# A hand-woven issue order against one computed by a list schedule in the builder and pinned

## The chip, the cores and the metric

The kernel runs on one core of one Trainium2 chip. The metric is the device time of one execution in microseconds, taken as the median over the runs of a kernel. Five engines matter here. PE does the matmuls, DVE (the vector engine) does element-wise work, ACT (the scalar engine) does copies and scaling, and POOL and SP mostly issue DMAs. Each engine works through its own list of instructions. So when the next instruction on the list has to wait, everything behind it waits too, ready or not. The Trainium skill, "Perfetto Trace Analysis", section "Per-engine timelines", says the same of ACT, DVE and POOL, whose queues it calls strict FIFO, and the traces here agree: one held list of ACT cost it 16.8 us.

## The reference, cut to what matters

```python
def reference(...):
    x = A_x                                            # 2048 x 1024
    g = sigmoid((x * gate_w).sum(-1, keepdims=True))
    a = _A_ref(x, ...)    # S5: a complex linear recurrence over 2048 steps,
                          #     h = Lam_bar * h + B_bar x,  y = 2 Re(C h) + x * Dskip
    b = _B_ref(x, ...)    # H3: kv = shift_conv(k) * v ; y = irfft(rfft(kv) * rfft(ssm_k))
                          #     + kv * ssm_D ; result q * y   (q is x)
    return g * a + (1 - g) * b
```

The kernel does the long convolution `b` with matmuls against sine and cosine tables, in eight rounds of 128 channels each. The recurrence `a` is done in four blocks of 512 time steps with eight groups of 128 states each, that is 32 units, called S5 units below.

## The kernel before

One round of the convolution goes through many hands. DVE prepares `kv` (shift convolution), a DMA stores and reloads it in another layout, PE does a first stage into PSUM, ACT copies that out as `zkv`, PE forms the spectrum, ACT copies it out as `kv`, DVE multiplies (`product`, result `pp`), PE transforms back (`inverse`), ACT copies that out as `qq`, 16 DMAs per round move `qq` into the layout `zb`, PE does a last stage (`final`), ACT copies it out as `cv`, and POOL stores it to `pB_scr` in memory. The S5 units are the filler that was put between these steps by hand:

```python
def evac(eng, o, i_, scale=None):            # copy a PSUM tile out
    if eng == "V":
        nc.vector.tensor_copy(o, i_)
    else:
        nc.scalar.copy(o, i_)
        todo = list(late); late.clear()
        for f in todo: f()                   # the zb stores wait for the next ACT copy

def zb_store(zb, qq, q):
    for i in range(4):
        k2 = 4 * q + i
        nc.scalar.dma_start(out=zb[k2:128:16]..., in_=qq[:, i]...)     # issued by ACT

# ... (cut: tables, parameters)
APU = [1, 2, 2, 2, 2, 2, 2, 3]               # S5 units per round, chosen by hand
for u in range(NU):                          # eight rounds
    na = 4 * APU[u]
    slots = [(i * na) // 12 for i in range(13)]
    # ... fill() advances the S5 stream by slots[pos+1]-slots[pos] steps
    if u > 0:
        # ... (cut)
        for q in range(4):
            stage1(ka, z, 0, q, "V" if q == 1 else "A")    # which engine copies: by hand
            if q == 1: fill()
        inverse(*pend, "A")
        # ... (cut)
    for q in range(4):
        spec(z, kv, q, 0, "A"); fill()
        spec(z, kv, q, 1, "A")
        pp_new = product(kv)
        next(kvg, None)                      # one step of the next round's kv
        if zb_prev is not None and q in (0, 1): final(zb_prev, u - 1, q, "A")
        if pend is not None: inverse(*pend, "A")
        pend = (pp_new, zb, q)
        fill()
# then the last part: C is transposed in and scaled (4 ACTIVATEs and 2 adds for each
# of 8 groups), S5 blocks 2 and 3, and 16 output tiles: 512 matmuls of 512 columns
```

Of the kernel before, what the change touches and what calls it, by code (L numbers as in the profile page):

```python
# [9 lines left out]
ALU = mybir.AluOpType  # L10
# [7 lines left out]
TB_MAX = 512  # L18


@with_exitstack
def kernel(
# [59 lines left out]

# [4 lines left out]
    bW = b.enter_context(tc.tile_pool(name="bW", bufs=1, side="right"))  # L87
    bpsum = b.enter_context(tc.tile_pool(name="bpsum", bufs=3, space=bass.MemoryType.PSUM))

# [28 lines left out]

    late = []

    def evac(eng, o, i_, scale=None):
        if eng == "V":
            nc.vector.tensor_copy(o, i_)
        else:
            nc.scalar.copy(o, i_)  # L125
            todo = list(late)
            late.clear()
            for f in todo:
                f()

    kv_tiles = {}

    def kv_load(job, pool):
        c0 = job * 128
        kT = pool.tile([128, S], BF16, name="kT")
        nc.sync.dma_start_transpose(out=kT, in_=kf[:, c0:c0 + 128])
        vT = pool.tile([128, S], BF16, name="vT")
        nc.sync.dma_start_transpose(out=vT, in_=vf[:, c0:c0 + 128])
        kv_tiles[job] = (kT, vT)

    def kv_steps(job, pool):
        c0 = job * 128
        kT, vT = kv_tiles.pop(job)
        acc = pool.tile([128, S], BF16, name="acc")
        nc.vector.tensor_scalar(out=acc, in0=kT, scalar1=skc[:, job, 0:1], scalar2=None, op0=ALU.mult)  # L145
        for j in range(1, KS):
            tmpj = pool.tile([128, S], BF16, name="tmpj")
            if j in (1,):
                nc.scalar.activation(out=tmpj[:, 0:S - j], in_=kT[:, 0:S - j], func=ACT.Identity,  # L149
                                     scale=skc[:, job, j:j + 1])  # L150
            else:
                nc.vector.tensor_scalar(out=tmpj[:, 0:S - j], in0=kT[:, 0:S - j], scalar1=skc[:, job, j:j + 1],
                                        scalar2=None, op0=ALU.mult)
            nc.vector.tensor_tensor(out=acc[:, j:S], in0=acc[:, j:S], in1=tmpj[:, 0:S - j], op=ALU.add)  # L154
            yield
        nc.vector.tensor_tensor(out=acc, in0=acc, in1=vT, op=ALU.mult)
        nc.gpsimd.dma_start(out=kv_scr[c0:c0 + 128, :], in_=acc)
        yield

    def load_A(src, u, name):  # L160
        t = bA.tile([128, NG, 128], BF16, name=name)
        nc.gpsimd.dma_start(out=t, in_=src[u * CH:(u + 1) * CH, :].rearrange("(g c) (n m) -> (c n) g m", c=8, m=128))
        return t

    def load_K(u):
        return load_A(B_ssm_k, u, "ka")

    def fix_K(u, ka):
        nc.vector.tensor_tensor(out=ka[:, :, 0], in0=ka[:, :, 0], in1=sdz[:, u * NG:(u + 1) * NG], op=ALU.add)  # L169

    def stage1(a, z, w, q, eng):
        ps = bpsum.tile([128, 4, 256], F32, name="ps")
        for i in range(4):
            nc.tensor.matmul(ps[:, i, :], lhsT=a[:, 4 * q + i, :], rhs=t1v, start=True, stop=True)  # L174
        evac(eng, z[:, :, w, :, 32 * q:32 * q + 32].rearrange("p k r (g c) -> p k r g c", c=8),
             ps.rearrange("p g (k r c) -> p k r g c", r=2, c=8))

    def spec(z, kv, q, h, eng):
        ps = bpsum.tile([128, 2, 2, 2, CH], F32, name="ps")
        for i in range(2):  # L180
            k2 = 4 * q + 2 * h + i
            nc.tensor.matmul(ps[:, i], lhsT=fC[:, k2, :], rhs=z[:, k2], start=True, stop=False)  # L182
            nc.tensor.matmul(ps[:, i, :, 0, :], lhsT=fS[:, k2, :], rhs=z[:, k2, :, 1, :], start=False, stop=False)  # L183
            nc.tensor.matmul(ps[:, i, :, 1, :], lhsT=fN[:, k2, :], rhs=z[:, k2, :, 0, :], start=False, stop=True)  # L184
        evac(eng, kv[:, 2 * h:2 * h + 2], ps)

    def product(kv):
        t1 = bW.tile([128, 4, 2, CH], BF16, name="t1")
        t2 = bW.tile([128, 4, 2, CH], BF16, name="t2")
        pp = bW.tile([128, 4, 2, CH], BF16, name="pp", bufs=2)  # L190
        nc.vector.tensor_tensor(out=t1, in0=kv[:, :, 0], in1=kv[:, :, 1], op=ALU.mult)
        nc.vector.tensor_tensor(out=t2[:, :, 0, :], in0=kv[:, :, 0, 0, :], in1=kv[:, :, 1, 1, :], op=ALU.mult)
        nc.vector.tensor_tensor(out=t2[:, :, 1, :], in0=kv[:, :, 0, 1, :], in1=kv[:, :, 1, 0, :], op=ALU.mult)
        nc.vector.tensor_tensor(out=pp[:, :, 0, :], in0=t1[:, :, 0, :], in1=t1[:, :, 1, :], op=ALU.subtract)
        nc.vector.tensor_tensor(out=pp[:, :, 1, :], in0=t2[:, :, 0, :], in1=t2[:, :, 1, :], op=ALU.add)  # L195
        return pp

    def zb_store(zb, qq, q):
        for i in range(4):
            k2 = 4 * q + i  # L200
            nc.scalar.dma_start(out=zb[k2:128:16].rearrange("s g r c -> s g (r c)"),  # L201
                                in_=qq[:, i].rearrange("p r c -> p (r c)"))

    def inverse(pp, zb, q, eng):
        ps = bpsum.tile([128, 4, 2, CH], F32, name="ps")
        for i in range(4):
            k2 = 4 * q + i
            nc.tensor.matmul(ps[:, i], lhsT=gC[:, k2, :], rhs=pp[:, i], start=True, stop=False)  # L208
            nc.tensor.matmul(ps[:, i, 0, :], lhsT=gN[:, k2, :], rhs=pp[:, i, 1, :], start=False, stop=False)  # L209
            nc.tensor.matmul(ps[:, i, 1, :], lhsT=gS[:, k2, :], rhs=pp[:, i, 0, :], start=False, stop=True)  # L210
        qq = bW.tile([128, 4, 2, CH], BF16, name="qq", bufs=2)
        evac(eng, qq, ps)
        late.append(lambda: zb_store(zb, qq, q))

    def final(zb, u, h, eng):
        ps = bpsum.tile([128, 2, 4, CH], F32, name="ps")
        for i in range(2):
            g0 = 8 * h + 4 * i
            nc.tensor.matmul(ps[:, i], lhsT=tFc, rhs=zb[:, g0:g0 + 4, 0, :], start=True, stop=False)
            nc.tensor.matmul(ps[:, i], lhsT=tFs, rhs=zb[:, g0:g0 + 4, 1, :], start=False, stop=True)  # L220
        cv = bW.tile([128, 8, CH], BF16, name="cv")
        evac(eng, cv, ps.rearrange("p a g c -> p (a g) c"))
        nc.gpsimd.dma_start(out=pB_v[:, 8 * h:8 * h + 8, u * CH:(u + 1) * CH], in_=cv)  # L223


    def load_BT(i):
        nc.sync.dma_start_transpose(out=BTre[i], in_=A_B_re[:, i * 128:(i + 1) * 128])
        nc.sync.dma_start_transpose(out=BTim[i], in_=A_B_im[:, i * 128:(i + 1) * 128])

    def load_xT(tbk, pool):  # L230
        xT_b = pool.tile([128, ND, TB], BF16, name="xT_b")
        for dt_ in range(ND):
            nc.sync.dma_start_transpose(out=xT_b[:, dt_, :],  # L233
                                        in_=xf[tbk * TB:(tbk + 1) * TB, dt_ * 128:(dt_ + 1) * 128])
        return xT_b

    def rot_table(pool, pi):
        ht = pool.tile([128, TB], F32, name="t1")
        nc.vector.tensor_scalar(out=ht, in0=iota_row, scalar1=col(thn, pi), scalar2=None, op0=ALU.mult)
        rq = pool.tile([128, TB], F32, name="t2")  # L240
        nc.vector.tensor_scalar(out=rq, in0=ht, scalar1=MAGIC, scalar2=-MAGIC, op0=ALU.add, op1=ALU.add)
        nc.vector.tensor_tensor(out=ht, in0=ht, in1=rq, op=ALU.subtract)
        nc.scalar.activation(out=rq, in_=ht, func=ACT.Abs)
        nc.scalar.activation(out=TBs[pi], in_=ht, func=ACT.Sin, scale=TWO_PI)
        nc.scalar.activation(out=TBc[pi], in_=rq, func=ACT.Sin, bias=pihalf_col, scale=-TWO_PI)

    def gates(tb, xT_b, psg):
        for tl in range(TT_B):
            for dt_ in range(ND):
                nc.tensor.matmul(psg[:, tl:tl + 1], lhsT=xT_b[:, dt_, tl * 128:(tl + 1) * 128],  # L250
                                 rhs=gwb[:, dt_:dt_ + 1], start=(dt_ == 0), stop=(dt_ == ND - 1))
        s_ = slice(tb * TT_B, (tb + 1) * TT_B)
        nc.scalar.activation(out=gcols[:, s_], in_=psg[:, 0:TT_B], func=ACT.Sigmoid)
        nc.scalar.activation(out=omg[:, s_], in_=psg[:, 0:TT_B], func=ACT.Sigmoid, scale=-1.0)

    hbs = {}
    inits = {}
    bus = {}
# [57 lines left out]
    def drain(gen):  # L316
        for _ in gen:
            pass
# [420 lines left out]
```

## Time and profile before

| | before |
|---|---|
| time, median of 2 runs | 642.45 us (641.56 to 643.35) |
| set-up (to the first spectrum matmul) | 56.3 us |
| middle (to the store of the last `pB_scr` tile) | 367.5 us |
| last part | 217.9 us |
| PE, DVE, ACT busy over the whole | 65%, 65%, 53% |

First come some lines of the page of the kernel before: the busy times, the busy tenths of PE and DVE in 40 slices of the span (9 means 90% or more), and at the end the chain of work that ended last, by engine.

```profile
span 641.7 us, 6317 instructions
...
PE 415.0 (65%) x2201; PEld 218.7 (34%) x2240; DVE 417.8 (65%) x741; ACT 340.2 (53%) x373; POOL 61.6 (10%) x86
...
PE   0204545746835844656876886245967797999996
...
DVE  4927574765964962766976765500999949888331
...
issue 40%; DVE 20%; PE 16%; DMA 10%; ACT 7%; POOL 2%; ACTq 2%; SPq 1%; POOLq 0%; DVEq 0%
```

DVE's row has no stretch of nines until the last part, and PE's only at the very end. In the chain the largest share is "issue", which is time in which an engine waited for nothing that the profile shows.

The table by windows cuts the span at the two landmarks given above. Its columns are the window, its length, then busy us and number of instructions for PE, the weight loads, DVE, ACT and POOL, then the granted clock, the DMA share and GB/s.

```profile
core 0: us, PE busy (x) PEld busy (x) DVE busy (x) ACT busy (x) POOL busy (x), PEclk, DMA share, GB/s
0.00:56.30 56.30, 8.86 (x65) 5.93 (x66) 33.06 (x76) 30.91 (x29) 10.63 (x17) 0.76 0.94 168
56.30:423.80 367.50, 224.93 (x1322) 133.70 (x1343) 241.96 (x435) 205.98 (x237) 32.93 (x36) 0.81 0.40 87
423.80:641.70 217.90, 181.24 (x815) 79.03 (x832) 142.78 (x230) 103.30 (x108) 18.05 (x33) 0.92 0.35 83
```

The set-up is bound by DMA (share 0.94). In the middle, DVE is the busiest engine, yet it is busy for only 241.96 of 367.5 us. So the length of the middle is DVE's work plus 125.5 us of DVE idleness. The same view cuts the last part into three stretches:

```profile
424.00:454.00 30.00, 19.05 (x77) 6.86 (x80) 5.75 (x9) 8.36 (x11) 6.06 (x11) 0.62 1.08 198
454.00:518.00 64.00, 49.51 (x207) 20.94 (x209) 62.88 (x107) 48.71 (x54) 2.15 (x4) 0.95 0.25 48
518.00:642.00 124.00, 112.68 (x535) 51.23 (x544) 74.15 (x115) 46.23 (x45) 9.67 (x18) 0.98 0.22 72
```

These are 30 us with DVE nearly idle and DMA at 1.08 (the share can come out slightly above 1 in a short window), 64 us with DVE full (62.88 busy), and 124 us with PE nearly full.

What DVE waited for in the middle is shown by the view of waits. Its columns are who waited for whom, then us in total, the number of times, and the longest.

```profile
engine line waited for: us in total, times, longest us
DVE acc L145 <- DMA kv_scr<-acc: 28.7, 6, 5.3
DVE ka L169 <- DMA ka<-in_B_ssm_k_dram: 25.9, 6, 6.6
DVE t_3068 L191 <- ACT kv L125: 6.1, 1, 6.1
```

The two largest waits are for DMA round trips: DVE may not start the next `acc` before the store of the last one has left the buffer, and it may not correct `ka` before its load has landed. The rest of the 125.5 us is scattered over many waits of about 6 us and less.

### The profile page before, as it was taken

The page shows a single profiled execution, that of the slowest core. Times are in us where ns is not written, and L with a number is a line of the kernel's source. Part 1 is how long each engine was busy: PE and PEld are TensorE (multiplying, and loading weights), DVE is VectorE, ACT ScalarE, POOL GpSimd, SP SyncE. Part 2 cuts the span into 40 slices and gives each one's busy share as a digit, 9 for nine tenths or more (in the row PEclk, how much of TensorE's full clock was granted, in tenths as well). Part 3 has the DMA queues.
Part 4 walks back from the last instruction along what each step waited for, and adds up shares of the span by engine and source line. Part 5 has one row for each costly group of instructions (what it writes and reads, how often), then busy time and mean ns, then how long its engine had stood idle before and what let it go on. Part 6 is the DMA issues. An engine that isn't in the chain of part 4 may idle for free.

```text
span 641.7 us, 6317 instructions
## 1 busy us (share of the span) xinstructions
PE 415.0 (65%) x2201; PEld 218.7 (34%) x2240; DVE 417.8 (65%) x741; ACT 340.2 (53%) x373; POOL 61.6 (10%) x86
## 2 busy tenths in 40 slices
PE   0204545746835844656876886245967797999996
PEld 0103224423523523434443543112422343444442
DVE  4927574765964962766976765500999949888331
ACT  2867934845645624846646663212888543433431
POOL 4100101101101101001101000040010011100000
PEclk9858687778967967789988978667897999899999
DMA  9992563263254246264233213389920033211211
GB/s 125 232 184 49 132 131 66 66 133 81 67 115 97 53 109 128 57 148 99 59 99 75 50 33 86 63 171 195 175 65 1 1 99 98 88 60 50 83 38 44
DMA packets 113799, 59.41 MB, mean 93 GB/s; under 512 B 89128, under 2 KB 105512, under 8 KB 113768
## 3 DMA queue, kind: packets, MB, share of 16 engines
q1 hardware_dynamic: 86784, 25.18, 20.3%
q0 software_dynamic: 7504, 25.44, 16.2%
q10 hardware_dynamic: 19480, 8.40, 6.0%
q8 instruction: 17, 0.28, 0.2%
q14 instruction: 14, 0.11, 0.1%
HBM read 17.06 MB, written 12.58 MB: 46 GB/s over the span
## 4 chain that ended last, share of the span: by engine, by line
issue 40%; DVE 20%; PE 16%; DMA 10%; ACT 7%; POOL 2%; ACTq 2%; SPq 1%; POOLq 0%; DVEq 0%
PE psy L648 12%; DMA kv_scr<-acc 6%; DVE W L287 4%; PE bu L266 3%; ACT zkv L125 2%; ACTq L201 2%; DVE acc L154 2%; SPq L233 1%; DMA kT<-in_B_k_dram 1%; DMA pB_scr<-cv 1%; PE ps L208 1%; ACT qq L125 1%; POOL pB_scr L223 1%; ACT cv L125 1%; DMA xT_b<-in_A_x_dram 1%
## 5 line engine op out<-in xcount | busy, mean ns | idle before, releaser
L125 ACT CAST kv<-ps 128x1024 bf16<-128x1024 f32 x64 | 63.2, 1018 | 33.9 <-DMA xT_b<-in_A_x_dram 16.8
L208 PE MATMUL ps<-pp,gC 128*128 128x256 bf16 x128 | 37.7, 320 | 65.7 <-DVE pp L195 53.4
L182 PE MATMUL ps<-zkv,fC 128*128 128x512 bf16 x118 | 49.6, 421 | 40.1 <-ACT zkv L125 25.9
L648 PEld LDWEIGHTS <-hb 128*128 128x128 bf16 x512 | 50.6, 99 | 73.3 <-issue 15.2
L125 ACT CAST zkv<-ps 128x1024 bf16<-128x1024 f32 x50 | 48.8, 1016 | 31.8 <-PE ps L174 23.3
L125 ACT CAST qq<-ps 128x1024 bf16<-128x1024 f32 x32 | 32.6, 1019 | 37.3 <-PE ps L210 37.2
L183 PE MATMUL ps<-zkv,fS 128*128 128x256 bf16 x128 | 38.5, 300 | 1.2 <-issue 0.9
L174 PE MATMUL ps<-tab_143,ka 128*128 128x256 bf16 x128 | 21.9, 331 | 26.2 <-DVE ka L169 19.8
L184 PE MATMUL ps<-zkv,fN 128*128 128x256 bf16 x128 | 38.6, 302 | 0.0
L125 ACT CAST bu<-bu 128x1024 bf16<-128x1024 f32 x32 | 32.2, 1007 | 11.4 <-DVE t_4049 L282 4.6
L266 PE MATMUL bu<-xT_b,BTre_68 128*128 128x512 bf16 x32 | 14.5, 453 | 35.8 <-ACT bu L125 17.6
L145 DVE TENSOR_SCALAR acc<-kT,skc 128x2048 bf16<-128x2048 bf16 x8 | 6.0, 753 | 44.6 <-DMA kv_scr<-acc 28.7
L208 PEld LDWEIGHTS <-gC 128*128 128x128 bf16 x128 | 14.3, 112 | 60.4 <-DVE pp L195 60.0
L660 ACT ACTIVATE pbb<-pbb,omg 128x1024 bf16<-128x1024 bf16 x16 | 18.3, 1147 | 30.3 <-DMA pbb<-pB_scr 21.1
L210 PE MATMUL ps<-pp,gS 128*128 128x128 bf16 x128 | 32.1, 251 | 0.0
L209 PE MATMUL ps<-pp,gN 128*128 128x128 bf16 x128 | 32.1, 250 | 0.0
L656 ACT ACTIVATE ga<-psy,gcols 128x1024 bf16<-128x1024 f32 x16 | 17.7, 1104 | 26.1 <-PE psy L648 26.1
L154 DVE TENSOR_TENSOR acc<-acc,tmpj 128x2047 bf16<-128x2047 bf16 (+2 forms) x24 | 29.2, 1217 | 2.9 <-ACT tmpj L149 2.8
L664 DVE TENSOR_TENSOR ot<-m_t,ga 128x1024 bf16<-128x1024 bf16 x16 | 11.0, 688 | 30.6 <-ACT ga L656 30.4
L287 DVE TENSOR_TENSOR_SCAN W<-rv,init_re,pre 128x512 bf16<-128x512 f32 x24 | 30.7, 1278 | 0.0
L287 DVE TENSOR_TENSOR_SCAN W<-rv,init_im,pre 128x512 bf16<-128x512 f32 x24 | 30.2, 1260 | 0.0
L659 ACT ACTIVATE m_t<-dsk,gcols 128x1024 bf16<-128x1024 bf16 x16 | 18.4, 1148 | 20.0 <-DVE ot L664 20.0
(706 smaller groups left out, 1154.2 us busy)
## 6 DMA issues: line engine op xcount, KB each, us to landing
zb<-qq ACTq DMA_DIRECT2D x128, 64.0 KB
ka<-in_B_ssm_k_dram POOLq DMA_DIRECT2D x8, 512.0 KB, 5.5
kv_scr<-acc POOLq DMA_DIRECT2D x8, 512.0 KB, 4.7
va<-kv_scr POOLq DMA_DIRECT2D x8, 512.0 KB, 5.5
pB_scr<-cv POOLq DMA_DIRECT2D x16, 256.0 KB, 3.5
x_tt<-in_A_x_dram POOLq DMA_DIRECT2D x16, 256.0 KB, 3.0
pbb<-pB_scr POOLq DMA_DIRECT2D x16, 256.0 KB, 3.0
out_dram<-ot SPq DMA_DIRECT2D x16, 256.0 KB
```

The lines of the kernel that those rows point to most:

```text
L125: nc.scalar.copy(o, i_)
L154: nc.vector.tensor_tensor(out=acc[:, j:S], in0=acc[:, j:S], in1=tmpj[:, 0:S - j], op=ALU.add)
L174: nc.tensor.matmul(ps[:, i, :], lhsT=a[:, 4 * q + i, :], rhs=t1v, start=True, stop=True)
L182: nc.tensor.matmul(ps[:, i], lhsT=fC[:, k2, :], rhs=z[:, k2], start=True, stop=False)
L183: nc.tensor.matmul(ps[:, i, :, 0, :], lhsT=fS[:, k2, :], rhs=z[:, k2, :, 1, :], start=False, stop=False)
L184: nc.tensor.matmul(ps[:, i, :, 1, :], lhsT=fN[:, k2, :], rhs=z[:, k2, :, 0, :], start=False, stop=True)
L208: nc.tensor.matmul(ps[:, i], lhsT=gC[:, k2, :], rhs=pp[:, i], start=True, stop=False)
L209: nc.tensor.matmul(ps[:, i, 0, :], lhsT=gN[:, k2, :], rhs=pp[:, i, 1, :], start=False, stop=False)
L210: nc.tensor.matmul(ps[:, i, 1, :], lhsT=gS[:, k2, :], rhs=pp[:, i, 0, :], start=False, stop=True)
L266: nc.tensor.matmul(ps[:, r, :], lhsT=BT[dt_][:, pi * 128:(pi + 1) * 128], rhs=xT_b[:, dt_, :], start=(dt_ == 0), stop=(dt_ == ND - 1))
L287: nc.vector.tensor_tensor_scan(out=W[:, r, :], data0=col(rv, pi).to_broadcast([128, TB]), data1=pre[:, r, :], initial=(0.0 if tb == 0 else ...
L648: nc.tensor.matmul(psy[:, dh, :], lhsT=hb[:, r, tl * 128:(tl + 1) * 128], rhs=CT[pi][:, dh * 512:(dh + 1) * 512], start=(pi == 0 and r == ...
```

## The change

The intent is to take the order out of the programmer's hands. Arithmetic, tiles and buffer counts stay. Each operation is described by the engines that may do it with an estimated cost, by what it reads and writes, and by a priority key (the round number with a fraction). A list scheduler in the builder then simulates the engines and buffers. It takes next whatever can start first, and among what can start within 0.1 us of that it takes the lowest key. The kernel's instructions are written out in that order, and at the end each instruction gets an ordering-only dependency on the one before it on the same engine. That last step is the pin. It is needed because the framework's own scheduler may otherwise move independent instructions of one engine past each other. The diff, cut to its core:

```diff
+class Planner:
+    DMA_RATE = 200e3
+    def start_of(self, o, e):                       # earliest start of op o on engine e
+        s = max([self.free.get(e, 0.0)] + [d.end for d in o.deps])
+        for t in o.w:                               # a new tile needs a free buffer
+            ...
+                if len(line) >= n:
+                    if line[-n].left: return None
+                    s = max(s, line[-n].end)
+        return s
+    def run(self, window=0.3, flex=0.0):
+        while ready:
+            ...
+            for e, c in by.items():
+                first = min(s for s, _ in c)
+                s, o = min(((s, o) for s, o in c if s <= first + window),
+                           key=lambda x: (x[1].key + (flex if ... e != next(iter(x[1].eng)) ...), x[1].n))
+                if pick is None or s < pick[0]: pick = (s, o, e)
+            s, o, e = pick
+            c = o.eng[e]
+            ...
+MM = {512: 0.216, 256: 0.108, 128: 0.062}           # us of a matmul by its columns
+def dma(q, kb):
+    return {q: (0.6, kb, 1.0)} if q != "POOL" else {q: (1.0, kb, 1.5)}
-def evac(eng, o, i_, scale=None):
+def evac(o, i_, r, w, cost=1.0, key=None):
+    ...
+    return op({ACTE: cost * 1.0, DVE: cost * 1.15}, fn, r, w, key=key)   # either engine
-            nc.scalar.dma_start(out=zb[k2:128:16]...
+            op(dma("SP", 64), lambda e, ...: nc.sync.dma_start(out=zb.ap[k2:128:16]...
-                nc.scalar.activation(out=t, in_=s_, func=ACT.Identity, scale=col(k_, pi))
+            op({ACTE: 0.98, DVE: 0.36}, f, [raw], [t])                   # C scaling
-    for u in range(NU):        # the hand-woven loop: slots, fill(), pend, late
-        ...
+    for u in range(NU):
+        base = KB0 + KBU * u                        # keys: round number, plus
+        ...
+        for q in range(4):
+            pl.key = base + 0.2 + 0.2 * q           # a fraction for each step
+            spec(...); spec(...); pp = product(kv); inverse(pp, zbs[u], q)
+    for tb in range(2):
+        base = KA0 + KAP * NP * tb                  # S5 units, at 0.4 rounds each
+        ...
+    t_end = pl.emit(window=0.1, flex=0.3)
+    ...
+    last = {}                                       # the pin
+    for ins in list(nc.cur_bb.bb.instructions):
+        prev = last.get(ins.engine)
+        if prev is not None:
+            tc.add_manual_dep(ins, prev.name, mybir.DependencyInfo(
+                mybir.DependencyClass.NoSync, mybir.DependencyReason.DATA), reason="order")
+        last[ins.engine] = ins
```

Three things move besides the order: the `zb` stores go from ACT to SP, PSUM copies may go to ACT or DVE as the planner finds best, and so may the scaling of C. (So may one small job, the first product of the shift convolution: 7 of its 8 instances stayed on ACT.)

## The prediction

> **What bounds the kernel now.** No engine is full: the page gives PE 65%, DVE 65%, ACT 53% of 641.7 us. The table by windows shows three regimes.
>
> - 0 to 56 us, set-up: DMA share 0.95; transposed loads fill the DMA engines.
> - 56 to 418 us, eight convolution rounds (about 46 us each) with S5 blocks woven in by hand: DVE 242 us busy of 362 (67%), ACT 205 (57%), PE 224 at a granted clock of 0.81, DMA 0.39. Nothing saturates; in-order waiting binds. The waits of 131 to 366 us: the inverse on DVE's product (35 us), the spectrum on ACT's zkv (19), ACT on the inverse (24). ACT's queue also issues the 128 zb stores at 0.61 us each, 78 us that the busy figure omits; one of them held ACT for 16.9 us behind the x transposes at 228 to 245.
> - 418 to 642 us: 30 us with DVE idle, DMA at 0.99 (x and C transposes); 64 us bound by DVE (63.3 busy); 130 us bound by PE (a 512-column matmul every 0.22 us, clock 0.98).
>
> **What changes.** Arithmetic, tiles and buffer counts stay. Every engine's order is computed greedily and pinned. PSUM copies can go to ACT (1.02 us) or DVE (1.22 us); C scaling, 32 x 1.15 us on ACT, can go to DVE (estimate 0.4 us, from the 0.75 us twice-as-wide scaling). The zb stores move to SP. The Trainium skill, "DMA: Bandwidth & Descriptors", section "Issuing engines are not separate DMA queues", says that the issuing engine saves only sequencer time; so the saving is ACT's 78 us, not bandwidth. The stores now queue behind SP's transposes, issued at 1.3 us each, sometimes stalling 2 to 5 us.
>
> **Cost.** Middle part: DVE+ACT+issue is 525 us on two engines now, 447 without the issues. DVE's fixed share is about 225 us, so the floor is near 230 us against 362. A greedy order should reach about 80%: 285 us, with some 15 us of tail after the S5 stream. Set-up stays DMA-bound, about 55 us. Last part: the C loads still wait for the tables' memory, so the 30 us gap stays nearly whole. PE needs 512 + 256 matmuls x 0.218 = 168 us there; if C is scaled 40 us in, out(0) can run under in(2): about 205 us against 224.
> Sum: 55 + 285 + 205 = 545. A frozen order amplifies wrong estimates: the planner costs a 512 matmul at 0.216 us where a slow clock gives 0.43, a transpose issue at 0.6 against 1.3, and knows no queue limits. I add 15 us: 560 us, range 530 to 605. Chances: faster 0.93, same 0.04, slower 0.03.
>
> **What would show it.** Round period falls from 46 to 35-38 us; DVE busy in the middle above 80%; no zb store left on ACT's queue; PSUM copies on DVE rise from 14 to several tens; the granted clock in the middle rises above 0.85 as PE idles less; a DVE gap of 20 us or more remains before the last part; PE near-saturated over the last 110 to 130 us.
>
> **What would make it wrong.** zb stores delayed behind transposes on SP, so that qq's two buffers hold ACT and the pinned order spreads this to PE and DVE: 3 to 5 us per round would cost up to 40 us. A pinned order that waits on a late DMA (C loads before out(0), va before stage 1) would show as one long wait on all engines. DVE overloaded by greedily taken copies would show as DVE above 95% with ACT below 50%. Upward surprise: set-up shortened by loading kv before B.

## The result, and the profile after

The kernel with the change took 549.96 us (median of 2 runs, 548.59 to 551.33) against 642.45 us. All ratios in this document are fast runs of one kernel against fast runs of the other in the same rounds, so they are not quite the ratio of the medians quoted. Here the ratio is 0.856 with a 95% interval of 0.8455 to 0.8665.

The lines of the page that answer to those of before:

```profile
span 549.6 us, 6362 instructions
...
PE 389.1 (71%) x2203; PEld 209.1 (38%) x2240; DVE 427.8 (78%) x758; ACT 310.5 (57%) x347; POOL 61.4 (11%) x85
...
PE   0024618877969678879787640766669999999996
...
DVE  4893978999989789899899810099999899997331
...
PE 40%; DVE 26%; DMA 12%; issue 7%; ACT 7%; SPq 6%; POOL 1%; ACTq 0%; DVEq 0%; POOLq 0%
```

DVE's row is now almost only sevens to nines from the fifth slice to 316 us, shortly before the middle ends (333.2 us), and the chain that ended last consists of work (PE 40%, DVE 26%) where it had consisted of "issue" (7%, from 40%). The table by windows, with the same landmarks:

```profile
0.00:52.60 52.60, 7.13 (x32) 4.47 (x33) 34.77 (x88) 30.05 (x34) 10.44 (x16) 0.83 1.06 165
52.60:333.20 280.60, 204.74 (x1357) 125.44 (x1377) 241.65 (x427) 189.98 (x218) 32.43 (x36) 0.90 0.51 112
333.20:549.60 216.40, 177.21 (x814) 79.21 (x830) 151.41 (x244) 90.49 (x95) 18.56 (x34) 0.91 0.38 89
```

| part | before | after | difference |
|---|---|---|---|
| set-up | 56.3 us | 52.6 us | -3.7 us |
| middle | 367.5 us | 280.6 us | -86.9 us |
| last part | 217.9 us | 216.4 us | -1.5 us |

So nearly all of the gain lies in the middle. DVE's busy time there is the same to within 0.3 us (241.96 and 241.65). What fell is its idle time, from 125.5 us to 280.6 - 241.65 = 38.9 us. That is 86.6 us less, which accounts for the whole difference of 86.9 us. Of the 38.9 us that are left, 15.7 are a tail from 317.5 us on, in which DVE has done its part of the rounds and already waits for the last part (12 us of the 125.5 were of that kind before); inside the rounds DVE is now idle for only about 23 us. The view of DVE's waits in the middle shows that the two large ones have gone or shrunk:

```profile
DVE z L385 <- PE ps L468: 6.2, 2, 4.1
DVE ka L459 <- DMA ka<-in_B_ssm_k_dram: 4.1, 3, 2.4
DVE kv L385 <- PE ps L482: 3.6, 3, 2.5
```

The wait for the store of `acc` (28.7 us) does not appear any more, although the tile still has one buffer, and the wait for `ka` fell from 25.9 to 4.1 us. The DMAs did not get faster; the landing of `ka` takes 6.8 us now and took 5.5 before. DVE has other work at the head of its list while they are under way.

In the last part the three stretches are these:

```profile
333.00:358.00 25.00, 11.14 (x63) 5.06 (x64) 0.01 (x1) 2.67 (x4) 6.76 (x12) 0.64 1.04 192
358.00:416.00 58.00, 38.61 (x172) 16.29 (x175) 57.45 (x96) 39.51 (x46) 2.15 (x4) 0.84 0.50 93
416.00:550.00 134.00, 127.66 (x583) 57.96 (x593) 93.96 (x149) 48.31 (x46) 9.66 (x18) 0.99 0.21 67
```

The stretch with DVE idle is still there. Two lines of the waits of the last part show it, and show something that the prediction had not seen:

```profile
DVE c_3356 L737 <- DMA CiT_3235<-in_A_C_im_dram: 40.4, 1, 40.4
...
PE bu L586 <- DVE ubu L385: 8.7, 1, 8.7
```

The pinned list of DVE has the scaling of C at its head at 317 us and stays there until the transposed C lands at 358 us. Behind it stands DVE's copy of a finished S5 result (`ubu`), for which PE waited 8.7 us. The finished result is only a small part of the wait, though: the matmuls of the first S5 unit started at 344 us, when the `xT` transposes had landed, so until then there was nothing to copy either. Ten row loads of 256 KB each went out on POOL from 337 us, beside the transposes of C; whether they delay those is tested in e8. C was completely scaled at 407 us, 74 us into the last part.

### The profile page after: what moved, and what is told of

Read it like the earlier page. It is cut to its first block, busy times and chain, and to the rows that moved or that the text cites. A ratio compares the mean times of both kernels' runs of the same rounds, so it can differ in the third digit from the quotient of the medians.

```text
span 549.6 us, 6362 instructions
## 1 busy us (share of the span) xinstructions
PE 389.1 (71%) x2203; PEld 209.1 (38%) x2240; DVE 427.8 (78%) x758; ACT 310.5 (57%) x347; POOL 61.4 (11%) x85
## 4 chain that ended last, share of the span: by engine, by line
PE 40%; DVE 26%; DMA 12%; issue 7%; ACT 7%; SPq 6%; POOL 1%; ACTq 0%; DVEq 0%; POOLq 0%
PE psy L764 20%; PE bu L586 9%; DVE W L602 4%; SPq L546 3%; DMA zb<-qq 3%; DMA CiT_3235<-in_A_C_im_dram 3%; PE ps L480 3%; SPq L515 2%; ACT z L387 2%; DVE acc L444 2%; PE ps L481 2%; PE ps L508 2%; PE ps L482 1%; DMA logdt_bf<-in_A_log_dt_dram 1%; DMA va<-kv_scr 1%
## 5 line engine op out<-in xcount | busy, mean ns | idle before, releaser
L387 ACT CAST z<-ps 128x1024 bf16<-128x1024 f32 x57 | 55.0, 1036 | 6.7 <-PE ps L468 6.4
L480 PE MATMUL ps<-z,fC 128*128 128x512 bf16 x115 | 48.9, 425 | 7.3 <-ACT z L387 5.7
L387 ACT CAST ubu<-bu 128x1024 bf16<-128x1024 f32 x28 | 28.2, 1007 | 24.6 <-PE bu L586 23.8
L481 PE MATMUL ps<-z,fS 128*128 128x256 bf16 x128 | 38.4, 300 | 1.3 <-issue 0.9
L482 PE MATMUL ps<-z,fN 128*128 128x256 bf16 x128 | 38.5, 301 | 0.0
L468 PE MATMUL ps<-tab_149,va 128*128 128x256 bf16 x128 | 19.2, 291 | 21.0 <-DMA va<-kv_scr 16.0
L737 DVE TENSOR_SCALAR c_3356<-CiT_3235,mc2i 128x1024 bf16<-128x1024 bf16 x1 | 0.5, 487 | 40.4 <-DMA CiT_3235<-in_A_C_im_dram 40.4
L532 POOL DMA_DIRECT2D pB_scr<-cv x16 | 14.3, 893 | 148.8 <-ACT cv L387 122.6
L444 DVE TENSOR_TENSOR acc<-acc,tmp 128x2047 bf16<-128x2047 bf16 (+2 forms) x24 | 29.1, 1214 | 0.8 <-ACT tmp L441 0.7
L757 ACT ACTIVATE pb<-pb,omg 128x1024 bf16<-128x1024 bf16 x16 | 18.3, 1144 | 17.7 <-DMA pb<-pB_scr 17.7
L387 ACT CAST cv<-ps 128x1024 bf16<-128x1024 f32 x15 | 15.2, 1015 | 22.7 <-PE ps L529 16.4
```

The source lines that it names most:

```text
L387: nc.scalar.copy(o(), i_())
L444: op({DVE: 1.15}, lambda e, t=t, tmp=tmp: tt(out=acc.ap[:, t:S], in0=acc.ap[:, t:S], in1=tmp.ap[:, 0:S - t], op=ALU.add), [tmp, acc], [acc])
L468: nc.tensor.matmul(ps.ap[:, i, :], lhsT=a.ap[:, 4 * q + i, :], rhs=t1v, start=True, stop=True)
L480: nc.tensor.matmul(o, lhsT=fC[:, k2, :], rhs=x, start=True, stop=False)
L481: nc.tensor.matmul(o[:, :, 0, :], lhsT=fS[:, k2, :], rhs=x[:, :, 1, :], start=False, stop=False)
L482: nc.tensor.matmul(o[:, :, 1, :], lhsT=fN[:, k2, :], rhs=x[:, :, 0, :], start=False, stop=True)
```

## The experiments

Twelve kernels were run. The median time before drifted between 643.73 and 648.16 us in these rounds, from chip to chip, so kernels of different rounds are compared by their ratios. A difference of ratios is turned into microseconds by multiplying by 643. The after kernel itself was not rerun in those rounds, so small differences (below about 0.01) from its ratio of 0.856 are not settled. One table gathers what the profiled runs say. Idle is the length of the middle less the busy time of DVE, by the windows view at each kernel's own landmarks.

| kernel | median us | ratio [95%] | middle | DVE busy | DVE idle | last part |
|---|---|---|---|---|---|---|
| before | 642.45 | 1 | 367.5 | 242.0 | 125.5 | 217.9 |
| after | 549.96 | 0.856 [0.8455, 0.8665] | 280.6 | 241.7 | 38.9 | 216.4 |
| e1_nopin | 659.55 | 1.0206 [1.0124, 1.0289] | 379.6 | 240.8 | 138.8 | 212.5 |
| e2_zbact | 588.33 | 0.9098 [0.9031, 0.9165] | 313.4 | 268.1 | 45.3 | 217.0 |
| e3_fixeng | 566.88 | 0.8733 [0.8642, 0.8824] | 296.4 | 238.8 | 57.6 | 218.2 |
| e4_before_zbsp | 664.38 | 1.0297 [1.0202, 1.0391] | 387.3 | 243.3 | 144.0 | 219.2 |
| e5_before_pin | 735.08 | 1.1415 [1.135, 1.1479] | 389.5 | 236.4 | 153.1 | 246.3 |
| e6_unit | 577.06 | 0.8952 [0.8906, 0.8997] | 303.9 | 253.6 | 50.3 | 215.7 |
| e7_cold | 633.11 | 0.9815 [0.9752, 0.9878] | 350.0 | 255.3 | 94.7 | 231.2 |
| e10_warm (profile slow) | 584.66 | 0.902 [0.8954, 0.9086] | 309.4 | 237.4 | 72.0 | 215.1 |
| e11_zbact_same | 567.16 | 0.8749 [0.8673, 0.8824] | 289.7 | 241.8 | 47.9 | 215.5 |
| e8_rows | 539.95 | 0.8381 [0.8318, 0.8444] | 281.4 | 242.0 | 39.4 | 208.0 |
| e9_cfirst | 543.43 | 0.8438 [0.8392, 0.8485] | 279.7 | 241.4 | 38.3 | 205.6 |
| e12_last_act | 548.32 | 0.8501 [0.8463, 0.854] | 286.9 | 241.9 | 45.0 | 212.3 |

All outputs are right. The questions were four: is it the planned order or the pin, what do the two moved jobs (stores, copies) give, how much do the planner's estimates matter, and why did the last part not shrink.

### 1. The planned order without the pin (e1_nopin)

```diff
-    last = {}
-    for ins in list(nc.cur_bb.bb.instructions):
-        ...
-            tc.add_manual_dep(ins, prev.name, ...)
-        last[ins.engine] = ins
```

> The changed kernel without the pinning edges: the planned emission stays, but the framework's own scheduler may reorder each engine again, as it did in the kernel before. If the planned order itself is what pays, the reordering loses a large part of the 92 us: I expect 580 to 625 us. If the gain comes from moving the zb stores off ACT's queue and from the choice of engine for the copies, it stays within 10 us of 550.

Measured: ratio 1.0206, slower than before by 1.2 to 2.9%. That is worse than the 580 to 625 us expected: the loss is more than the whole 92 us. The framework put the instructions in another order than the planner's. (About 690 of the 4482 instructions on PE and 270 of the 760 on DVE stand elsewhere.) The windows of the middle show what that did. First all engines, then only the line that ends an S5 unit (its count is the number of units finished, one counted twice where a window cuts it):

```profile
core 0: us, PE busy (x) PEld busy (x) DVE busy (x) ACT busy (x) POOL busy (x), PEclk, DMA share, GB/s
100.00:200.00 100.00, 61.76 (x336) 32.44 (x340) 81.50 (x135) 44.47 (x55) 7.05 (x6) 0.87 0.42 73
200.00:300.00 100.00, 55.80 (x348) 32.83 (x353) 84.59 (x146) 49.64 (x56) 10.36 (x11) 0.88 0.42 95
300.00:443.00 143.00, 78.81 (x490) 47.80 (x498) 43.12 (x89) 72.56 (x75) 14.23 (x15) 0.73 0.34 77
```

```profile
core 0: us, DVE busy (x), PEclk, DMA share, GB/s
100.00:200.00 100.00, 3.79 (x9) 0.87 0.42 73
200.00:300.00 100.00, 2.98 (x8) 0.88 0.42 95
300.00:443.00 143.00, 0.00 (x0) 0.73 0.34 77
```

All sixteen S5 units of the middle (3.79 + 2.98 = 6.77 us, at 0.42 us each) were done before 300 us. Until then DVE was busy for 81% and 85% of the time. Afterwards there was no filler, and DVE was busy for 43.12 of 143 us, waiting on the chain of the convolution (the line is for the whole middle; 50.1 us of it, in 7 waits, come after 300 us):

```profile
DVE t L492 <- ACT kv L387: 64.7, 11, 17.9
```

What follows: the plan is worth nothing here if it is not pinned. In this run the reordering used up the filler early.

### 2. The pin without the plan (e5_before_pin)

```diff
         drain(out_block(3))
+        last = {}
+        for ins in list(nc.cur_bb.bb.instructions):
+            ...   # the same pin, on the hand-written program order
```

> The kernel before with the pinning edges of the change, so that every engine keeps the hand-written program order. Rival 'pin alone' (the framework's reordering spoils the hand order, and pinning is the whole gain): 550 to 600 us. Theory 'planned order': the hand order was written to be reordered, so pinning it gains nothing: 630 to 720 us.

Measured: ratio 1.1415, the slowest of all and slower than both forecasts. The loss lies in all three parts: 41 us in the set-up, 22 in the middle, 28 in the last part. The first spectrum matmul came at 97.7 us where it comes at 56.3 us in the kernel before, and DVE waited 108.5 us in 23 pieces for ACT's copies of `kv`. So the time of the kernel before already owed something to the framework's reordering of the hand-written program; by this run it was worth about 0.14 x 643 = 91 us. A pin by itself does harm, and so does a plan by itself. The gain belongs to the pair. It can't be divided between the two.

### 3. The zb stores (e4_before_zbsp, e2_zbact, e11_zbact_same)

In the kernel before, ACT issues 128 `zb` stores at 0.61 us each. One of them is seen to do harm in the timeline, whose columns are start, us, engine and instruction, and in the waits:

```profile
227.31 17.69 ACTq L201 DMA_DIRECT2D zb<-qq  x4
```

```profile
ACT kv L125 <- DMA xT_b<-in_A_x_dram: 16.8, 1, 16.8
```

This group of four stores stretches over 17.69 us although no single issue takes more than 1.2 us. ACT's list was held among them, and ACT stood still for 16.8 us until, as the profile infers, an `xT` transpose of SP had landed. The instruction records of the trace show why. The stores of ACT and the DMAs of SP take turns on the same eight completion semaphores. The fourth store takes the one that the second of the `xT` transposes had just used, and so waits, from 229.5 to 244.4 us, until that transpose has landed. SP itself had been held, from 228.7 to 240.6 us, by a wait for PE before the first of these transposes. So the tie between the two lists is of the program's making. Three kernels ask what the move to SP is worth.

```diff
# e4: before, with the stores on SP
-            nc.scalar.dma_start(out=zb[k2:128:16]...
+            nc.sync.dma_start(out=zb[k2:128:16]...
# e2: after, with the stores on ACT, and the planner knows it
-            op(dma("SP", 64), lambda e, i=i, k2=k2: nc.sync.dma_start(
+            op({ACTE: (0.6, 64, 1.0)}, lambda e, i=i, k2=k2: nc.scalar.dma_start(
# e11: after, with the stores issued by ACT, but planned as if by SP
-            op(dma("SP", 64), lambda e, i=i, k2=k2: nc.sync.dma_start(
+            op(dma("SP", 64), lambda e, i=i, k2=k2: nc.scalar.dma_start(
```

> The kernel before with only the zb stores moved from ACT's queue to SP's. Rival 'queue': most of the gain, 560 to 590 us. Theory 'order': ACT was not full, so 620 to 640 us, mostly from the 17 us in which a store held ACT behind the x transposes.

Measured: ratio 1.0297, slower; both forecasts missed. But this run is confounded: after the move the framework put other instructions in another order too (about 520 of 4482 on PE and 180 of 743 on DVE stand elsewhere). It shows that the move alone does not bring the gain. It does not measure the move.

> The changed kernel with the 128 zb stores back on ACT's queue (the planner is told of their 0.6 us). Theory 'order': DVE is the full engine in the middle part and ACT has slack (57% busy), so 78 us of issue on ACT costs little: 550 to 565 us. Rival 'queue': the 78 us that left ACT are the gain; then this gives most of it back, 600 us or more.

Measured: 588.33 us, between the two forecasts; ratio 0.9098, or 0.0538 x 643 = 35 us slower than after. The listing of one engine's copies tells why it is so much. DVE's copies out of PSUM in e2, then in the kernel after (durations are min/median/max in ns, then first and last start):

```profile
L385 DVE CAST kv<-ps x19: 1200/1221/1226, 56.1 to 347.3; 128x1024 bf16<-128x1024 f32 x19
...
L385 DVE CAST z<-ps x13: 1201/1218/1226, 31.1 to 332.3; 128x1024 bf16<-128x1024 f32 x13
```

```profile
L385 DVE CAST z<-ps x7: 1214/1224/1225, 30.3 to 193.0; 128x1024 bf16<-128x1024 f32 x7
L385 DVE CAST kv<-ps x7: 1200/1225/1226, 56.0 to 311.7; 128x1024 bf16<-128x1024 f32 x7
```

Over all tiles, DVE made 47 such copies in e2 and 25 in after; in the middle 39 and 17. The planner saw ACT loaded with stores and gave 22 more copies to DVE, at 1.22 us each 27 us. DVE's busy time in the middle rose by nearly that, from 241.65 to 268.1 us, and DVE is the engine that bounds the middle. Its idle time hardly changed (45.3 against 38.9 us).

> The changed kernel with its plan unchanged (the planner still believes that the zb stores are SP's) but the stores issued from ACT at the planned places. e2, where the planner knew, lost 38 us, with 23 more copies pushed to DVE. If the issue time on ACT is the cost, ACT (190 us busy of 281 in the middle) takes 78 us more and the frozen order passes it on: 585 to 620 us. If e2's loss was only the re-planning onto DVE: 550 to 565 us.

Measured: 567.16 us, at the edge of the lower forecast (562 by the ratio); ratio 0.8749, or 12 us slower than after, give or take 8 by the two intervals. Here the built kernel has the same instructions in the same order on PE and DVE as after; only the issuing engine of the stores differs. So in a planned order the move of the stores is worth about 12 us of the 92, and the rest of e2's loss came from the plan's answer to it. That the loss is smaller than the 78 us of issue time fits ACT's slack: it is busy 190 of 281 us in the middle.

### 4. Free choice of engine (e3_fixeng)

```diff
-        return op({ACTE: cost * 1.0, DVE: cost * 1.15}, fn, r, w, key=key)
+        return op({on: cost * (1.15 if on == DVE else 1.0)}, fn, r, w, key=key)
...
-            op({ACTE: 0.98, DVE: 0.36}, f, [raw], [t])
+            op({ACTE: 0.98}, f, [raw], [t])
```

The copies were fixed to the engines that the kernel before uses, and the C scaling to ACT. One job (the first product of the shift convolution) had to stay free, since the planner otherwise ran into a state without a free buffer.

> The changed kernel with copies and C scalings tied to the engines of the kernel before (all on ACT but one in eight stage-1 copies on DVE; the planner plans with that). Theory 'order': 550 to 565 us, since only 25 copies sat on DVE and 14 did before; the C scaling on ACT may cost up to 10 us in the last part. Rival 'balance': 580 us or more.

Measured: 566.88 us, at the edge of the lower forecast (561 by the ratio); ratio 0.8733, or 11 us slower than after, with overlapping intervals. The profile points the same way: the middle is 15.8 us longer, with DVE 2.9 us less busy and 18.7 us more idle. So the free choice brings perhaps 10 to 15 us. Since DVE was less busy and not more, it probably does so by giving a waiting copy to whoever is free rather than by balancing the load.

### 5. The planner's estimates (e6_unit, e7_cold, e10_warm)

```diff
# e6: every compute operation is planned as 1.0 us
+                c = 1.0
                 self.free[e] = s + c
# e7: matmuls planned at twice, e10: at half the duration
-    MM = {512: 0.216, 256: 0.108, 128: 0.062}
+    MM = {512: 0.432, 256: 0.216, 128: 0.124}     # e7
+    MM = {512: 0.108, 256: 0.054, 128: 0.031}     # e10
```

> The changed kernel, but the planner believes that every compute operation takes 1.0 us on whatever engine (transfers as before). If good durations are what makes the order good: 580 us or more, because matmul groups of 0.4 us and scans of 1.2 us look alike and copies look cheaper on DVE than they are. If tracking dependencies and buffers is enough, in whatever units: below 570 us.

Measured: 577.06 us, between the two forecasts; ratio 0.8952, or 25 us slower than after. A plan that knows dependencies, buffers and transfers but no durations of compute operations still keeps about 67 of the 92 us.

> The changed kernel with the planner's matmul costs doubled, as at half clock. I had added 15 us in the prediction for a frozen order made from wrong estimates, the matmul first. If that mattered, the doubled cost changes the time by more than 2% in one direction. If DVE binds the middle part whatever PE is said to cost: 540 to 562 us.

Measured: ratio 0.9815, or 81 us slower than after; nearly the whole gain is gone. In the middle the plan of e7 spends DVE's work in the first half (161.23 of 178.1 us busy) and starves it in the second (94.04 of 171.9):

```profile
51.90:230.00 178.10, 112.61 (x697) 67.63 (x696) 161.23 (x253) 95.62 (x112) 18.59 (x21) 0.85 0.55 114
230.00:401.90 171.90, 114.13 (x683) 65.77 (x681) 94.04 (x185) 84.49 (x96) 13.77 (x14) 0.83 0.30 64
```

The planner's own sums suggest why. The planner of e7 counts 364 us of work for PE up to the end of the middle, against 260 for DVE; in the kernel after it counts 184 for PE and 249 for DVE. The plan of e7 then serves PE, which is not the engine that bounds the middle, and DVE's work is put wherever it suits PE. This reading was not tested by itself, and the next run shows that it can't be the whole story.

> The changed kernel with the planner's matmul costs halved. e7 (doubled) lost 83 us because the plan then served PE, which is not the full engine. If an error only hurts when it names the wrong bottleneck, halving is harmless: 540 to 565 us. If any wrong figure hurts (a frozen order amplifies errors): 580 us or more.

Measured: ratio 0.902, or 30 us slower than after; its row in the table is read with care. Costs that are too low leave DVE looking like the bottleneck, so by the explanation of e7 they should be harmless (the first forecast, 540 to 565 us). That missed; the time fell at the edge of the second forecast (580 us or more). DVE's busy time in the profile is low (237.4 us) and its idle time high, so the loss is again idleness of DVE. In the middle it waited 16.7 us for loads of `ka` (4.1 in after) and 14.1 us in three waits for PE before copies of `cv` tiles, and the set-up took 61.1 us. Why a matmul that looks too cheap leads to that was not settled.

A related point: the durations the planner assumes are those of PE at full clock, and PE had run at 0.81 in the middle before. Under the plan PE idles less and the granted clock in the middle rose to 0.90. The Trainium skill, "TensorE: Matmul & The Clock Gate", Part 1, says that the clock is halved when PE has been idle and full after sustained work. The trace agrees: in the kernel after, PE stood idle for 8.7 us before 362 us, the next matmuls of 512 columns start 0.427 us apart for about 4 us, and those after them 0.216 us apart. So the planner's 0.216 us was more nearly true under the plan than in the kernel before.

### 6. The last part (e8_rows, e9_cfirst, e12_last_act)

The first theory about the last part was that the row loads delay the transposes of C, and with them the pinned head of DVE's list.

```diff
# e8: row loads behind the transposes, on the same queue
-        pl.key = k0 - 0.8
-        op(dma("POOL", 256), lambda e: nc.gpsimd.dma_start(out=x.ap, ...
-        op(dma("POOL", 256), lambda e: nc.gpsimd.dma_start(out=pb.ap, ...
+        pl.key = k0 - 0.05
+        op(dma("SP", 256), lambda e: nc.sync.dma_start(out=x.ap, ...
+        op(dma("SP", 256), lambda e: nc.sync.dma_start(out=pb.ap, ...
```

> The changed kernel with the row loads of the last part (x and pb, ten of 256 KB at once) issued on SP behind the C transposes instead of at once on POOL. Theory: they delay the first C tiles for which DVE stands still by its frozen order; then the DVE gap before the last part falls from 40 to about 30 us and the time to 537 to 545 us. Rival: the gap is set by the xT load and the memory that C waits for; then 547 to 553 us.

Measured: ratio 0.8381, 12 us better than after's 0.856, with intervals that just do not overlap; the theory's forecast was met. The middle is unchanged (281.4 against 280.6 us), the last part is 208.0 against 216.4 us, and DVE's long wait is shorter by 12.9 us (it was 40.4):

```profile
DVE c L737 <- DMA CiT<-in_A_C_im_dram: 27.5, 1, 27.5
```

C is scaled at 397 us where it was 407. This is the best version found; it beats both kernels. The next step was to hurry C still more:

```diff
# e9: e8, and the scaling of C gets the lowest keys, its transposes their measured cost
-        pl.key = 0.1 + 0.1 * pi
+        pl.key = 0.01 * pi
-            op(dma("SP", 256), lambda e, CT=CT, src=src: ...
+            op({"SP": (1.3, 256, 1.0)}, lambda e, CT=CT, src=src: ...
```

> The changed kernel with the row loads behind the C transposes (as in e8) and, in the plan of the last part, the C scaling ahead of S5 block 2 from its second tile on, with a transpose issue costed at the measured 1.3 us. In e8 the C tiles had landed at about 361 us but were all scaled only at 397, because DVE, full from 349 on, alternated with block 2, and PE got its 111 us of output matmuls late. If the last part is a race of PE's 168 us against the moment C is ready, PE is busy some 15 to 25 us earlier: 520 to 532 us. If DVE's total (154 us) or the x transposes bind instead: 536 to 545 us.

Measured: 543.43 us, ratio 0.8438 [0.8392, 0.8485], the same as e8 within the intervals. The theory that C's readiness sets the end missed: C was scaled at 388 us, 9 us sooner than in e8, and the last part is only 2.4 us shorter. The other forecast was met. The windows of the last part show DVE nearly full until 450 us and PE full from 400 us:

```profile
400.00:450.00 50.00, 49.74 (x229) 22.68 (x232) 49.19 (x84) 20.42 (x22) 0.00 (x0) 1.00 0.26 80
450.00:500.00 50.00, 49.79 (x229) 22.66 (x232) 41.34 (x64) 19.12 (x19) 0.00 (x0) 1.00 0.22 74
500.00:537.00 37.00, 32.18 (x147) 14.46 (x148) 9.01 (x13) 9.95 (x9) 0.00 (x0) 0.98 0.12 43
```

It seems that when C is ready sooner, other work of DVE is only later. That suggested the rival, that DVE's 152 us of work bound the last part, and it was tested by taking 11 us of work from DVE:

```diff
# e12: e8, and in the last part S5's copies and the scaling of C only on ACT
-        evac(lambda: bu.ap, lambda: ps.ap, [ps], [bu])
+        evac(lambda: bu.ap, lambda: ps.ap, [ps], [bu], both=tb < 2)   # else ACT alone
-            op({ACTE: 0.98, DVE: 0.36}, f, [raw], [t])
+            op({ACTE: 0.98}, f, [raw], [t])
```

> The version with the row loads behind the C transposes (539.95 us, 0.8381 of before), and on top of it, in the last part alone, the PSUM copies of S5 and the C scaling only on ACT. In that version the last part had 5 such copies (6.1 us) and 10 scalings (4.9 us) on DVE, so 11 us of DVE's 152.6 us go to ACT, which is busy 90 us of 207 there. Theory 'DVE binds the last part': DVE is full from 349 to 490 us, so 11 us less on it should end the part earlier: 529 to 536 us, ratio 0.82 to 0.832, middle unchanged at about 280 us. Rival 'PE binds it once C is scaled': PE was busy 100 of 100 us from 400 to 500 and the end is set by when the first out product may start (397 us); the scaling on ACT takes 32 x 1.14 = 36 us from about 350, so C is ready no earlier than about 390 and the time stays within 3 us of 540: ratio 0.834 to 0.843. If the greedy planner makes something worse of it: over 545.

Measured: 548.32 us (8 runs, 545.88 to 554.0), ratio 0.8501 [0.8463, 0.854], slower than e8 by 8 us by the ratios. So neither theory's forecast was met, but the third ("over 545"). In the profile the last part is 4.3 us longer than in e8. The rest lies before it, where PE, DVE and ACT have the same instructions in the same order as in e8, so it is variation between runs or chips (the profiled run was the slowest of the eight). DVE was 8.5 us less busy in the last part (144.07 against 152.60) and the part was still not shorter. Two lines of the waits:

```profile
DVE wt L596 <- ACT ubu L387: 32.1, 2, 30.1
...
PE psy L764 <- DVE CrT L742: 9.6, 3, 4.8
```

The first is for the most part the old gap at the start of the part under another name: 30.1 of the 32.1 us, before DVE's first S5 step, where e8 shows 27.5 us before its first scaling of C. The second says that C was late. With the scaling on ACT alone, C was ready 70 us into the last part, against 65 us in e8 and 75 us in after. In these three kernels the part ends 142 to 143 us after C is ready. So e12 took work from DVE and delayed C at once, and its 4.3 us are about the 5 us by which C came later. It does not settle whether DVE's total binds, and it fits the theory that C's readiness sets the end; what speaks against that theory alone is e9, where the part ends 149 us after C. PE is full from 400 us on in e8 and e9 and DVE nearly so until 450. Whether a better order exists for this part stays open. The wait for the transposes of C at its start (27.0 us on DVE in e9) was not removed by any run. A second buffer for `xT`, to bring block 2 in early, did not fit in on-chip memory.

## Why the prediction was right, and where its sum was off

The measured 549.96 us lies in the range of 530 to 605 and 10 us below the central 560. Its steps, one by one:

- **"In-order waiting binds" the middle: right.** DVE's busy time in the middle did not change (241.96 and 241.65 us), and its idle time fell from 125.5 to 38.9 us, which is the gain. Experiments 1, 2 and 5 show that the idleness follows order and pin: 138.8 us unpinned, 153.1 with the hand-written order pinned, 94.7 with wrong matmul costs, all at about the same DVE work (236 to 255 us).
- **Set-up about 55 us: right** (52.6), still at a DMA share of 1.06.
- **Middle 285 us: right** (280.6). DVE reached 86% against "about 80%", with a tail of 15.7 us ("some 15 us"). That the sum came out so near is in part luck: DVE had 242 us of work and not the floor of 230, and the better share made up for it. Further signs came true: round period 280.6 / 8 = 35.1 us as predicted (35 to 38), the granted clock 0.90 as predicted (above 0.85), and no `zb` store left on ACT's queue (the queue that had moved 8.40 MB moved 0.01 MB).
- **"The saving is ACT's 78 us": right in kind, mis-sized if read as time.** The Trainium skill, "DMA: Bandwidth & Descriptors", section "Issuing engines are not separate DMA queues", says that another issuing engine saves only sequencer time, usually little beside the DMA. With identical lists on PE and DVE, e11 puts that saving at about 12 us. The prediction used the 78 us only in the floor and did not add them to the gain.
- **PSUM copies on DVE from 14 "to several tens": too high.** There are 25, of which 17 in the middle, so DVE's work there hardly changed. More would not have helped: e2, where it took 47, was 35 us slower than after.
- **Last part 205 us "if C is scaled 40 us in": this is the term of the sum that was mis-sized.** It measured 216.4 us. C was scaled 74 us in. The prediction had the DVE gap right in kind ("20 us or more remains") but not that the pinned list would hold a finished S5 copy behind it (PE waited 8.7 us for that copy), nor that the row loads would delay the transposes (e8 gets 8.4 us of the last part back by moving them).
- **"I add 15 us" for wrong estimates: not needed in this kernel.** The risk is real (25, 81 and 30 us in e6, e7 and e10). That it cost nothing here fits the granted clock of 0.90 in the middle, at which most matmuls do take the planned time, but no run shows this by itself. This error of 15 us and the error of 11 us in the last part nearly cancelled, so it is luck that the total came out only 10 us from the central forecast.

## What to carry to other kernels

When no engine is full and the gaps of the busiest engine are scattered over many releasers, the order of the lists is the suspect: compare the busiest engine's busy time with the length of the part, for the difference is the most that an order can win. A computed order paid here only when it was also pinned against the framework's own scheduler; each half alone was slower than the hand-woven kernel. Check the planner's durations of every engine against a trace, not only of the one that binds: wrong matmul costs lost 30 and 81 of the 92 us although PE did not bind the middle, while planning all compute operations alike lost 25. When an experiment moves work from one engine to another, check what else it delays, as e12 delayed C. In a pinned list, check each DMA wait at the head of the binding engine's list for finished work standing behind it, and keep that engine's load low before balancing the others.

## What the Trainium skill lacked or had wrong

- "Perfetto Trace Analysis", section "Optimization Strategy", says to find the gaps on the most-contended engine and to determine what blocks there. This is the method used here and it works, but it lacks the case in which the blocking is the list order itself. DVE's gap of 28.7 us behind the store of `acc` vanished with the same DMA and the same single buffer, only by giving DVE other work first.
- "DMA: Bandwidth & Descriptors", section "Issuing engines are not separate DMA queues", calls the sequencer time of issuing a DMA usually small. 128 stores at 0.61 us held ACT's sequencer for 78 us in sum, and moving them was worth about 12 us. Nor does the section count what a store costs the issuing engine's list when it must first wait for a completion semaphore that another engine's DMA has used: once ACT stood still for 16.8 us for that reason.
- The same page, section "DMA Transpose (X-bar)", gives no cost for issuing a transpose of this size on this chip. The traces show about 1.26 us for each of the `xT` transposes (median, 24 of them in the kernel after), twice the 0.60 us of a plain store on the same engine.
- No page says what it can cost in time that the order on an engine is not the order of the program. Without the pin the same planned program was 1.0206 of before, with it 0.856; with its hand-written order pinned, the kernel before was 1.1415.
- "TensorE: Matmul & The Clock Gate", Part 1, agrees with the traces (0.427 and 0.216 us between matmuls of 512 columns), but does not draw the consequence for the cost table of a planner: planning with twice the full-clock figure cost 81 us here, and with half of it 30 us.
